# Values of the second tile ahead of the first up product, scores of the third tile behind the second: an attention and feed-forward kernel on one core

## The chip, the cores and the metric

The kernel runs on one core of a Trainium2 chip. The core has a matrix engine (TensorE, "PE" in the profile, its weight loads "PEld"), a vector engine (VectorE, DVE), an activation engine (ScalarE, ACT), a general engine (GpSimd, POOL) and a queue engine (SyncE, SP); 16 DMA engines move data. The metric is the device time of the program in microseconds (us). Before the change its median over 13 runs was 210.06 us (209.4 to 212.1).

## The reference

Chunked attention with a little context and eight memory slots, and behind it a layer norm and a two-layer feed-forward block with a residual:

```python
# q, k, v: (4, 8, 768, 64); mem_k, mem_v: (4, 8, 8, 64)
for c in range(24):                                    # chunks of 32 queries
    k_ctx = k[:, :, max(0, 32*c - 16) : min(768, 32*c + 40)]     # 16 left, 8 right; v_ctx alike
    k_full = concatenate([mem_k, k_ctx]); v_full = concatenate([mem_v, v_ctx])
    a = softmax(q_c @ k_full.T / 8)
    out[:, :, 32*c : 32*c + 32] = a @ v_full
x = out.transpose(0, 2, 1, 3).reshape(4, 768, 512)     # heads side by side
xn = (x - mean(x)) / sqrt(var(x) + 1e-6) * g_ln
return x + maximum(xn @ w_ch1, 0) @ w_ch2              # w_ch1 512 x 2048, w_ch2 2048 x 512
```

## The kernel before

**Tiles.** A tile is 128 rows of one batch element with all eight heads, so there are six tiles to a batch element and 24 in all, written `(b, t)`. Three tiles make a unit `u` of the feed-forward part (8 units). W1 and W2 lie in four quarters each (`w1c[0..3]`, `w2c[0..3]`).

**Steps of one tile.** `scores` (L319) does 16 small matmuls of keys (`KT`) against queries (`QR`) into an `att` slot of PSUM. `soften` (L335), twice, is the exponential on ScalarE into `AT`. `weigh` (L349) does 16 matmuls of `AT` with `V` into an `att` slot, with a column of ones that gives the sums of the softmax; `gather` (L361) takes reciprocals and scales on VectorE into `xs`, with the row sum beside it, and makes the negative mean; `values` (L345) is `weigh` and then `gather`. `norm` (L374) makes `xn` on VectorE. `turn_x` (L395) transposes `xn` on TensorE and copies it into `xT` with VectorE. `stats` and `root` find the reciprocal deviation, which is applied at the very end. `up_tile` (L453) multiplies one tile with one quarter of W1, `up_two` (L439) two tiles at once with one quarter, in two PSUM slots; `relu` (L420) takes each product out on ScalarE or VectorE. `down` (L470) multiplies with W2.

**Keys.** `transpose_block` brings a block of 256 keys, turned, into PSUM. `window` (L218) copies the piece of it that one group of 64 keys sees into `KT`, in two halves; pieces are numbered 0 to 3. Block 1 of batch element 0 (`K1`, L694) lies in the PSUM bank `mm[2]`. `key_left` (L199) copies the left context of a group from the group ahead of it. `half_q` and `part_q` turn half a block of queries and copy it to `QR`; `mix_q` (L285) puts the raw queries in order on VectorE beforehand. `v_mem` (L142) puts the memory values into `V`. `warm` (L591) issues matmuls on zeros that nobody uses.

**Order.** The order of each engine's instructions is written out by hand, and each engine follows it; a wait comes in only where data or a buffer is needed. PSUM slots of one kind are taken in turn (`slot`, L87): four of `mm`, two of `att`. The first unit starts by hand, in the lines that the change touches; from `plan` on (L776) steps are put on a time table. Behind the changed lines come: `up_two(0, 2)` with the third quarter, the products of tile 2 alone, and the loads' last parts.

**Loads.** POOL's queue issues nearly all loads, in the order of L662 to L690: `load_v(b, g)` one of twelve pieces of V, `load_w1(c)` a quarter of W1, `load_q(0, 1, h)` half a block of queries in two transfers. POOL's loads use eight semaphores in turn: a load waits until the eighth load before it has landed. SP's queue carries the transposing DMAs (`cross`, L306, and `turn_x` of most tiles) and the stores.

Of the kernel before, what the change touches and what calls it, by code (L numbers as in the profile page):

```python
# [15 lines left out]
def kernel(  # L16
# [67 lines left out]
    mm = [ps.tile([128, 512], FP32, name=f"mm{i}") for i in range(4)]  # L84
    turn = {"att": 0, "mm": 0}

    def slot(kind):  # L87
        lst = {"att": att, "mm": mm}[kind]
        turn[kind] = (turn[kind] + 1) % len(lst)
        return lst[turn[kind]]  # L90

    def dram(t, offset, pattern):
        return bass.AP(tensor=t.tensor, offset=offset, ap=[list(p) for p in pattern])

    def free(ap, off, pattern, parts=None):
        p = list(ap.ap[0]) if parts is None else [ap.ap[0][0], parts]
        return bass.AP(tensor=ap.tensor, offset=ap.offset + off, ap=[p] + [list(x) for x in pattern])

    def as16(t):
        return t.bitcast(FP16)  # L100

    def copy(eng, out, in_):
        if eng is nc.scalar:
            eng.copy(out=out, in_=in_)  # L104
        else:
            eng.tensor_copy(out=out, in_=in_)  # L106

    dve, act, pool = nc.vector, nc.scalar, nc.gpsimd
# [26 lines left out]
    def load_v(b, g):  # L135
        lo, hi = 16 if g == 0 else 0, 80 if g == NG - 1 else 96
        nc.gpsimd.dma_start(  # L137
            out=V[b % 2][lo:hi, g, :, 0:64],
            in_=dram(v, b * H * HS + (64 * g - 16 + lo) * D, [[64, hi - lo], [HS, H], [1, 64]]),
        )  # L140
# [7 lines left out]
    def load_w1(c):  # L148
        nc.gpsimd.dma_start(
            out=w1c[c], in_=dram(moe_w_ch1, 512 * c, [[FF, 128], [128 * FF, 4], [1, 512]])  # L150
        )
# [47 lines left out]
    def key_left(b, g, eng):  # L199

        copy(eng, free(KT[b % 2], GW * g, [[W, 4], [1, 16]]),
             free(KT[b % 2], GW * (g - 1) + 64, [[W, 4], [1, 16]]))
# [15 lines left out]
    def window(b, blk, banks, k0, eng):  # L218

        for half in ((0, 1) if eng is dve else (1, 0)):  # L220
            key_piece(b, banks[half], 4 * blk + k0, *PIECES[k0], eng, half)
# [63 lines left out]
    def mix_q(b, blk, half, eng):  # L285
        rows = slice(64 * half, 64 * half + 64)
        s, o = pick(st, ("b", b, blk, 1))[rows, :], pick(iv, ("b", b, blk, 1))[rows, :]
        copy(eng, free(o, 0, [[64, 2], [128, 8], [1, 64]]), s)
# [30 lines left out]
    def scores(b, t):  # L319
        p = slot("att")  # L320
        score_slot[b, t] = p
        for gg in range(2):
            for j in range(4):
                for par in range(2):
                    rows = slice(64 * par, 64 * par + 64)
                    nc.tensor.matmul(  # L326
                        out=p[:, par, (4 * gg + j) * 64 : (4 * gg + j) * 64 + 64],
                        lhsT=free(KR[b % 2][rows, :], GW * (2 * t + gg) + W * j, [[1, 128]]),
                        rhs=free(QR[b % 2][rows, t // 2, :, :], 8 * gg +
                                 (32 * j + 16 * (t % 2) if (b, t) >= (1, 4) else 64 * (t % 2) + 16 * j),  # L330
                                 [[128, 8], [1, 8]]),
                        start=True, stop=True, tile_position=(64 * par, 0),
                    )

    def soften(b, t, c):  # L335
        p = score_slot[b, t]
        nc.scalar.activation(  # L337
            out=free(AT[t % 3], 32 * c, [[64, 16], [1, 32]]),
            in_=free(p, 4 * c, [[64, 16], [1, 4], [8, 8]], W),
            func=ACTF.Exp, bias=band[0:W, c : c + 1], scale=0.125,  # L340
        )
# [3 lines left out]
    def values(b, t):  # L345
        weigh(b, t)
        gather(b, t)

    def weigh(b, t):  # L349
        p = value_slot[b, t] = slot("att")  # L350
        for par in range(2):
            for j in range(4):
                for gg in range(2):
                    nc.tensor.matmul(  # L354
                        out=p[64 * gg : 64 * gg + 64, par, 128 * j : 128 * j + HD],
                        lhsT=AT[t % 3][:, par, gg, j, :],
                        rhs=V[b % 2][:, 2 * t + gg, 4 * par + j, 0:HD],
                        start=(j == 0), stop=(j == 3), tile_position=(0, 64 * gg),
                    )

    def gather(b, t):  # L361
        p, r, x = value_slot[b, t], rec[t % 2], xs[(NT * b + t) % 9]
        nc.vector.reciprocal(out=r, in_=free(p, 64, [[128, 8]]))
        nc.vector.scalar_tensor_tensor(  # L364
            out=x.rearrange("p (h d) -> p h d", h=8),
            in0=free(p, 0, [[128, 8], [1, 64]]), scalar=1.0,
            in1=free(r, 0, [[1, 8], [0, 64]]),
            op0=ALU.mult, op1=ALU.mult, accum_out=tot[t],
        )
        nc.vector.tensor_scalar(  # L370
            out=nmean[t], in0=tot[t], scalar1=-1.0 / 512, scalar2=None, op0=ALU.mult
        )

    def norm(b, t, gb=gb):  # L374
        i = NT * b + t
        nc.vector.scalar_tensor_tensor(  # L376
            out=xn[i % 4], in0=xs[i % 9], scalar=nmean[t], in1=gb, op0=ALU.add, op1=ALU.mult,
        )
# [16 lines left out]
    def turn_x(b, t):  # L395
        i = NT * b + t
        dst = xT[(i // 3) % 2][:, :, 128 * (i % 3) : 128 * (i % 3) + 128]
        if i not in ON_PE:
            nc.sync.dma_start_transpose(out=dst, in_=xn[i % 4])
            return  # L400
        p = slot("att")
        pv = as16(p[:, 0, :])
        for dt in range(4):
            nc.tensor.matmul(  # L404
                out=pv[:, 128 * dt : 128 * dt + 128],
                lhsT=xn[i % 4][:, 128 * dt : 128 * dt + 128], rhs=identity,
                is_transpose=True, start=True, stop=True,
            )
        nc.vector.tensor_copy(out=dst, in_=free(pv, 0, [[128, 4], [1, 128]]))
# [29 lines left out]
    def up_two(u, c, engs):  # L439

        for m, eng in engs:
            p = slot("mm")
            for k_ in range(2):
                for dt in range(4):
                    nc.tensor.matmul(
                        out=p[:, 256 * k_ : 256 * k_ + 256],
                        lhsT=free(w1c[c][:, dt, :], 2 * m + k_, [[4, 128]]),
                        rhs=xT[u % 2][:, dt, 0:256],
                        start=(k_ == 0 and dt == 0), stop=(k_ == 1 and dt == 3),
                    )  # L450
            relu(eng, rT[c][:, 2 * m : 2 * m + 2, 0:256], free(p, 0, [[256, 2], [1, 256]]))

    def up_tile(u, c, i, eng):  # L453
        p = slot("mm")
        for k_ in range(4):
            for dt in range(4):
                nc.tensor.matmul(
                    out=p[:, 128 * k_ : 128 * k_ + 128],
                    lhsT=free(w1c[c][:, dt, :], k_, [[4, 128]]),
                    rhs=xT[u % 2][:, dt, 128 * i : 128 * i + 128],  # L460
                    start=(k_ == 0 and dt == 0), stop=(k_ == 3 and dt == 3),
                )
        pair = rT[c][:, :, 128 * i : 128 * i + 128], free(p, 0, [[128, 4], [1, 128]])
        if eng is None:
            return pair
        relu(eng, *pair)
# [124 lines left out]
    def warm(n, m=512, p=None):  # L591
        p = mm[3] if p is None else p
        for _ in range(n):
            nc.tensor.matmul(out=p[:, 0:m], lhsT=zero[:, 0:128], rhs=zero[:, 0:m], start=True, stop=True)
# [66 lines left out]

    load_v(0, 0)  # L662
    load_v(0, 1)
    load_w1(0)
    load_q(0, 1, 0)
    load_v(0, 2)
    load_v(0, 3)
    load_w1(1)
    load_v(0, 4)
    load_v(0, 5)  # L670
# [23 lines left out]
    K1 = [as16(mm[2])[:, 512 * h : 512 * h + 512] for h in range(2)]  # L694
# [46 lines left out]
    copy(act, gb, mm[3])  # L741
    warm(4, 512, mm[1])
    turn_x(0, 0)
    mix_q(0, 1, 0, dve)
    window(0, 1, K1, 0, act)
    window(0, 1, K1, 1, act)
    window(0, 1, K1, 2, dve)
    key_left(0, 4, dve)
    turn["mm"] = 3
    late = up_tile(0, 0, 0, None)  # L750
    Q1 = as16(slot("mm"))
    half_q(0, 1, 0, Q1)
    part_q(0, 1, 0, Q1, act)
    warm(1, 512, mm[3])
    scores(0, 2)
    values(0, 1)
    norm(0, 1)
    soften(0, 2, 0)
    soften(0, 2, 1)
    window(0, 1, K1, 3, act)  # L760
    warm(5, 512, mm[3])
    turn_x(0, 1)
    relu(dve, *late)
    v_mem(0, 4, 6, dve)
    total(cnt[:, 1:2], 0, 80)
    total(cnt[:, 2:3], 96, W)
    nc.vector.tensor_tensor(out=cnt[:, 1:2], in0=cnt[:, 1:2], in1=cnt[:, 2:3], op=ALU.add)
    up_tile(0, 0, 1, act)
    values(0, 2)
    up_two(0, 1, ((0, act), (1, act)))  # L770
    norm(0, 2)
    turn_x(0, 2)
    up_two(0, 2, ((0, act), (1, act)))
# [190 lines left out]
```

## Time and profile before

| What | us |
|---|---|
| median of 13 runs (range) | 210.06 (209.4 to 212.1) |
| the profiled execution, its span | 212.1, 210.3 |
| TensorE busy | 199.0 |
| VectorE busy | 163.1 |
| ScalarE busy | 109.9 |
| POOL busy | 110.3 |

All times inside the profile count from the start of the span. A timeline row gives the start, the busy time of a group of equal instructions, engine, line, operation, output and inputs, shapes and the number of instructions; in brackets the engine's idle time ahead of it and what ended it. Groups of several matmuls are pipelined, so the end of a group is a little behind the start of the next. A row of stages gives start and end, the length, the busy time of PE, PEld, DVE, ACT and POOL with the number of instructions, the granted clock of TensorE, the share of the DMA engines and their GB/s.

### The profile page before, as it was taken

The numbers are of one execution on the slowest core, as the hardware profiler recorded it, in microseconds if no ns is written. First come the engines' busy times: TensorE is split into PE (matmuls) and PEld (weight loads), VectorE is DVE, ScalarE is ACT, GpSimd is POOL, SyncE is SP. The second block draws the span as 40 slices with busy tenths as digits, with TensorE's granted clock in tenths as the row PEclk, the third lists the DMA queues.
The fourth block names the chain that finished last, engine by engine and source line by source line (L and its number), as shares of the span: only waits on it lengthen the run. The fifth ranks groups of instructions, "written<-read, shape, count | busy, mean of one in ns | idle before, by whom it ended". The sixth has DMA issues, their size and how long they took to land.

```text
span 210.3 us, 5284 instructions
## 1 busy us (share of the span) xinstructions
PE 199.0 (95%) x2045; PEld 135.0 (64%) x2045; DVE 163.1 (78%) x402; ACT 109.9 (52%) x238; POOL 110.3 (52%) x189
## 2 busy tenths in 40 slices
PE   7776999999999999989999999999999999999992
PEld 2454895547765467566666866586658766776581
DVE  5985836598989999968598999995897679565654
ACT  2764369637786077807693176737770566022300
POOL 7975787899789999733667893400040013000000
PEclk9999999999999999999999999999999999999999
DMA  5999999999999979998999999996022211220012
GB/s 157 200 193 191 212 198 185 202 148 235 162 131 155 184 160 129 130 157 227 162 152 171 95 199 131 117 199 154 1 48 79 100 27 28 78 100 0 0 53 100
DMA packets 74099, 28.11 MB, mean 134 GB/s; under 512 B 62169, under 2 KB 70105, under 8 KB 74074
## 3 DMA queue, kind: packets, MB, share of 16 engines
q0 software_dynamic: 46336, 14.71, 68.8%
q1 hardware_dynamic: 27594, 12.80, 28.9%
q10 hardware_dynamic: 144, 0.26, 0.5%
q8 instruction: 16, 0.26, 0.5%
q14 instruction: 9, 0.07, 0.1%
HBM read 30.28 MB, written 6.29 MB: 174 GB/s over the span
## 4 chain that ended last, share of the span: by engine, by line
PE 67%; DVE 5%; DMA 5%; ACT 2%; issue 1%; DVEq 0%
PE mm L430 33%; PE mm L475 14%; PE mm L522 13%; DMA QR<-iv 5%; PE att L354 3%; DVE osb L538 3%; PE att L326 2%; ACT AT L337 1%; DVE xs L364 1%; DVE KT L106 1%; PE att L404 1%; DVE three L492 0%; PE mm L233 0%; PE att L233 0%; ACT rT L422 0%
## 5 line engine op out<-in xcount | busy, mean ns | idle before, releaser
L430 PE MATMUL mm<-xT,w1c 128*128 128x384 f16 x464 | 81.1, 327 | 0.0
L422 ACT ACTIVATE rT<-mm 128x384 f16<-128x384 f32 (+1 forms) x78 | 38.6, 499 | 55.1 <-PE mm L430 48.4
L430 PEld LDWEIGHTS <-w1c 128*128 128x128 f16 x464 | 51.0, 114 | 21.1
L475 PE MATMUL mm<-w2c,rT 128*128 128x512 f16 x192 | 44.4, 379 | 0.0
L137 POOL DMA_DIRECT2D V<-in_v_dram x48 | 38.5, 809 | 5.0 <-DMA V<-in_v_dram 2.0
L424 DVE TENSOR_SCALAR rT<-mm 128x384 f16<-128x384 f32 (+1 forms) x47 | 26.1, 560 | 15.0 <-PE mm L430 11.8
L337 ACT ACTIVATE AT<-att,band 104x512 f16<-104x512 f32 x48 | 31.1, 686 | 3.4 <-PE att L326 3.2
L475 PEld LDWEIGHTS <-rT 128*128 128x128 f16 x192 | 18.2, 98 | 19.5
L387 POOL TENSOR_SCALAR veps<-sq 128x1 f32<-128x1 f32 x24 | 7.8, 327 | 43.3 <-ACT junk L381 21.3
L522 PEld LDWEIGHTS <-SA 128*128 128x128 f16 x184 | 17.9, 98 | 3.4 <-DVE SA L492 1.4
L381 ACT ACTIVATE junk<-xs,nmean 128x512 f16<-128x512 f32 x24 | 17.3, 720 | 4.5 <-issue 1.8
L123 POOL DMA_DIRECT2D st<-in_q_dram x28 | 16.2, 597 | 4.2 <-DMA st<-in_q_dram 2.0
L391 POOL TENSOR_TENSOR rstd<-veps,mhalf 128x1 f32<-128x1 f32 x24 | 16.5, 686 | 2.0
L364 DVE SCALAR_TENSOR_TENSOR xs<-att,rec 128x512 f32<-128x512 f32 x24 | 16.6, 692 | 0.9
L376 DVE SCALAR_TENSOR_TENSOR xn<-xs,nmean,gb 128x512 f16<-128x512 f32 x23 | 16.6, 747 | 0.2
L522 PE MATMUL mm<-T,SA 128*128 128x256 f16 x144 | 16.7, 273 | 0.0
L522 PEld LDWEIGHTS <-rT 128*128 128x128 f16 x144 | 14.1, 98 | 3.2 <-issue 0.3
L104 ACT COPY KT<-rawk 128x352 f16<-128x352 f16 (+2 forms) x14 | 10.3, 783 | 7.1 <-DMA rawk<-iv 7.1
L129 POOL DMA_DIRECT2D st<-in_k_dram x22 | 12.8, 592 | 0.8 <-DMA w2c<-in_moe_w_ch_dram 0.8
L522 PE MATMUL mm<-w2c,rT 128*128 128x256 f16 x96 | 12.4, 273 | 0.0
L106 DVE COPY iv<-st 128x1024 f16<-128x1024 f16 (+1 forms) x23 | 10.3, 454 | 1.9 <-DMA QR<-iv 1.6
L106 DVE COPY V<-memv 8x2560 f16<-8x2560 f16 (+1 forms) x14 | 10.8, 774 | 0.4
(107 smaller groups left out, 232.4 us busy)
## 6 DMA issues: line engine op xcount, KB each, us to landing
out_dram<-osb SPq DMA_DIRECT2D x23, 256.0 KB, 2.3
V<-in_v_dram POOLq DMA_DIRECT2D x40, 96.0 KB, 5.9
st<-in_k_dram POOLq DMA_DIRECT2D x22, 128.0 KB, 5.2
w1c<-in_moe_w_ch_dram POOLq DMA_DIRECT2D x4, 512.0 KB, 8.1
st<-in_q_dram POOLq DMA_DIRECT2D x32, 64.0 KB, 4.9
w2c<-in_moe_w_ch_dram POOLq DMA_DIRECT2D x4, 512.0 KB, 8.7
st<-in_q_dram POOLq DMA_DIRECT2D x6, 128.0 KB, 8.1
V<-in_v_dram POOLq DMA_DIRECT2D x8, 80.0 KB, 5.4
```

The costliest lines, as they stand in the source:

```text
L106: eng.tensor_copy(out=out, in_=in_)
L137: nc.gpsimd.dma_start(out=V[b % 2][lo:hi, g, :, 0:64], in_=dram(v, b * H * HS + (64 * g - 16 + lo) * D, [[64, hi - lo], [HS, H], [1, 64]]),)
L337: nc.scalar.activation(out=free(AT[t % 3], 32 * c, [[64, 16], [1, 32]]), in_=free(p, 4 * c, [[64, 16], [1, 4], [8, 8]], W), func=ACTF.Exp, ...
L364: nc.vector.scalar_tensor_tensor(out=x.rearrange("p (h d) -> p h d", h=8), in0=free(p, 0, [[128, 8], [1, 64]]), scalar=1.0, in1=free(r, 0, ...
L376: nc.vector.scalar_tensor_tensor(out=xn[i % 4], in0=xs[i % 9], scalar=nmean[t], in1=gb, op0=ALU.add, op1=ALU.mult,)
L381: nc.scalar.activation(out=junk, in_=xs[(NT * b + t) % 9], func=ACTF.Square, bias=nmean[t], scale=1.0, accum_out=sq[t],)
L391: nc.gpsimd.tensor_tensor(out=rstd[(NT * b + t) % 9], in0=veps[t % 3], in1=mhalf, op=ALU.pow)
L422: nc.scalar.activation(out=o, in_=p, func=ACTF.Relu)
L424: nc.vector.tensor_scalar(out=o, in0=p, scalar1=0.0, scalar2=None, op0=ALU.max)
L430: nc.tensor.matmul(out=p, lhsT=free(w1c[c][:, dt, :], i, [[4, 128]]), rhs=xT[u % 2][:, dt, 128 * lo : 128 * (lo + n)], start=(dt == 0), st ...
L475: nc.tensor.matmul(out=p, lhsT=rT[c][:, k_, 128 * i : 128 * i + 128], rhs=w2c[c][:, k_, :], start=(c == 0 and k_ == 0), stop=(c == 3 and k ...
L522: nc.tensor.matmul(out=p, lhsT=left(h)[:, k_, :], rhs=right(h)[:, k_, :], start=(h == 0 and k_ == 0), stop=(h == 1 and k_ == 3),)
```

## The change

Tile 1's V loads (pieces 2 and 3) are issued ahead of the first quarter of W1 and of the queries. On TensorE tile 1's `weigh` comes right after the transpose of tile 0, ahead of tile 0's up product; its `gather` and `norm` follow on VectorE directly after `mix_q`. The six filler matmuls around become three. `turn_x(0, 1)` comes ahead of tile 2's scores. Window 2 of block 1 and `key_left` move behind the copy of `turn_x(0, 1)` on VectorE, and window 3 on ScalarE comes ahead of tile 2's softens. Tile 2's scores and softens move behind tile 1's up product. `values(0, 2)` moves behind `up_two(0, 1)`, whose second relu moves from ScalarE to VectorE. Nothing else is changed, and what is computed is the same.

```diff
     load_v(0, 0)
     load_v(0, 1)
+    load_v(0, 2)
+    load_v(0, 3)
     load_w1(0)
     load_q(0, 1, 0)
-    load_v(0, 2)
-    load_v(0, 3)
     load_w1(1)
...
     turn_x(0, 0)
+    weigh(0, 1)
     mix_q(0, 1, 0, dve)
+    gather(0, 1)
+    norm(0, 1)
     window(0, 1, K1, 0, act)
     window(0, 1, K1, 1, act)
-    window(0, 1, K1, 2, dve)
-    key_left(0, 4, dve)
     turn["mm"] = 3
     late = up_tile(0, 0, 0, None)
     Q1 = as16(slot("mm"))
     half_q(0, 1, 0, Q1)
     part_q(0, 1, 0, Q1, act)
-    warm(1, 512, mm[3])
-    scores(0, 2)
-    values(0, 1)
-    norm(0, 1)
-    soften(0, 2, 0)
-    soften(0, 2, 1)
+    warm(3, 512, mm[3])
+    turn_x(0, 1)
+    window(0, 1, K1, 2, dve)
+    key_left(0, 4, dve)
     window(0, 1, K1, 3, act)
-    warm(5, 512, mm[3])
-    turn_x(0, 1)
     relu(dve, *late)
     v_mem(0, 4, 6, dve)
...
     up_tile(0, 0, 1, act)
+    scores(0, 2)
+    soften(0, 2, 0)
+    soften(0, 2, 1)
+    up_two(0, 1, ((0, act), (1, dve)))
     values(0, 2)
-    up_two(0, 1, ((0, act), (1, act)))
     norm(0, 2)
     turn_x(0, 2)
     up_two(0, 2, ((0, act), (1, act)))
```

## The prediction, made before the changed kernel ran

> **What bounds the kernel now.** I read the shares by engine first, then busy time by stage, then the timeline of the stage that the edit touches, then TensorE's later waits.
>
> ```profile
> PE 199.0 (95%) x2045; PEld 135.0 (64%) x2045; DVE 163.1 (78%) x402; ACT 109.9 (52%) x238; POOL 110.3 (52%) x189
> ...
> 15.00:22.00 7.00, 4.89 (x81) 3.43 (x81) 4.43 (x13) 3.39 (x10) 4.30 (x8) 1.00 1.45 195
> 22.00:30.00 8.00, 7.82 (x115) 7.32 (x114) 4.49 (x13) 4.17 (x7) 6.22 (x9) 1.00 1.36 204
> ```
>
> The second and third lines are stages (start:end, length, then busy us of PE, PEld, DVE, ACT, POOL, the clock, DMA). From 22 us on PE is full, and it does its instructions in the order written. So what counts is when it begins the unbroken stretch: I take the start of `up_two(0, 2)`, the second group of L445, as the marker. Whatever delays it delays the rest, unless a later wait of PE swallows it. Behind the first 15 us only the stage to 22 us has holes to speak of, 2.1 us of them, and 1.6 us of what is busy are filler matmuls (L594).
>
> ```profile
> 14.41 0.39 PE L404 MATMUL att<-identity,xn 128*128 128x128 f16 x4
> 14.83 0.42 DVE L409 COPY xT<-att 128x512 f16<-128x512 f16 x1 [0.26 <-PE att L404]
> 15.31 1.05 PE L457 MATMUL mm<-xT,w1c 128*128 128x128 f16 x16 [0.52 <-DVE xT L409]
> 16.20 0.59 DVE L106 COPY KT<-mm 128x176 f16<-128x176 f16 x2 [0.49 <-ACT KT L104]
> 17.37 0.41 PE L326 MATMUL att<-QR,KT 64*128 64x64 f16 x16 [0.35 <-ACT QR L104]
> 17.71 0.44 PE L354 MATMUL att<-V,AT 104*64 104x65 f16 x16
> 18.23 0.21 DVE L363 RECIPROCAL rec<-att 128x8 f32<-128x8 f32 x1 [1.35 <-PE att L354]
> 18.98 0.48 ACT L104 COPY KT<-mm 128x160 f16<-128x160 f16 x2
> 20.20 0.40 PE L404 MATMUL att<-identity,xn 128*128 128x128 f16 x4 [0.86 <-DVE xn L376]
> 21.19 1.08 PE L457 MATMUL mm<-xT,w1c 128*128 128x128 f16 x16 [0.59 <-DVE xT L409]
> 22.30 0.44 PE L354 MATMUL att<-V,AT 104*64 104x65 f16 x16
> 22.68 1.94 PE L445 MATMUL mm<-xT,w1c 128*128 128x256 f16 x16
> 22.79 0.21 DVE L363 RECIPROCAL rec<-att 128x8 f32<-128x8 f32 x1
> 24.77 0.40 PE L404 MATMUL att<-identity,xn 128*128 128x128 f16 x4
> 25.00 1.91 PE L445 MATMUL mm<-xT,w1c 128*128 128x256 f16 x16
> ```
>
> Two chains are to be seen. Tile 1: values on PE (17.71), then VectorE's reciprocal to `xn` (18.23 to 20.14, 1.91 us), transpose (20.20), copy, up product (21.19). PE has little but filler meanwhile. Tile 2: the same chain, from 22.30 to the transpose at 24.77, has the 1.94 us of `up_two(0, 1)` laid over it, so PE loses only about 0.3 us. The 16.20 row is one more reading: VectorE's window copy waited for ScalarE's, which reads the same PSUM bank.
>
> ```profile
> 83.22 2.51 SPq L309 DMA_TRANSPOSE QR<-iv  x1
> ...
> 93.07 0.43 DVE L106 COPY iv<-st 128x1024 f16<-128x1024 f16 x1 [1.63 <-DMA QR<-iv]
> ...
> 94.75 1.05 PE L522 MATMUL mm<-w2c,SA 128*128 128x256 f16 x8 [1.08 <-DVE SA L492]
> ...
> 99.42 0.29 PE L326 MATMUL att<-QR,KT 64*128 64x64 f16 x8 [0.35 <-DVE KT L106]
> ```
>
> These are the places where a shift could shrink: a transposing DMA that took 9.73 us holds VectorE, and PE then waits 1.08 and 0.35 us (0.16 us besides, at 62.67, for ScalarE, which is itself paced by PE).
>
> **The loads.** V loads 2 and 3 go ahead of W1's first quarter and the two loads of q. POOL's issue times (0.79 each) put W1(0) at 5.74 + 1.57 = 7.31 us, the q loads at 8.1; from W1(1) on the order is as before. The five transfers landed at 13.04 (W1(0)), 13.5 and 13.83 (q), 14.4 and 14.9 (V). They follow each other closely, so I take the stream as the limit: V 2 and 3 now land near 11.3, W1(0) 1.07 later, at 14.1, and q last, at 14.9. The other end is the issue delay itself: 14.6 and 15.4. W1(0) is wanted at 15.34, q by `mix_q` at 15.29. Cost: nothing, at most 0.15 us on VectorE; the cover is the wait for `xT`, and without it all later starts move one for one. POOL's loads wait each for the eighth before: W1(2) now waits for V 2 instead of W1(0), so it is issued about 1.5 us before 13.38. It landed at 21.3 behind W1(1) and V 4 and 5 (18.7), and PE wants it at 25: no gain, and no loss. W1(3) still waits for W1(1). SP's queue is not touched.
>
> **Tile 1's values forward.** `weigh(0, 1)` needs tile 1's weights, which ScalarE ends at 14.91: 14.96 to 15.34, before `up_tile(0, 0, 0)`, which started at 15.31 anyway: 0.03 us. VectorE does the copy of `xT` to 15.25 and `mix_q` to 15.71, then tile 1's chain, 1.91 us: `xn` at 17.65 instead of 20.14. PE does up product, `half_q` and three fillers (to about 17.4), transposes at 17.71, and the copy of `xT` begins 0.51 us later (20.20 to 20.71), at 18.22. A lead of 2.49 us so far; three fillers fewer (0.7 us) are part of it, not added to it.
>
> **The moved windows.** `window(0, 1, K1, 2)` and `key_left` now stand behind that copy on VectorE. K1 lies in mm[2], the bank that `up_tile(0, 0, 1)` takes. So PE must wait for window 3 on ScalarE, and window 3 for window 2 on VectorE, as the 16.20 row shows for one bank. 18.22 + 0.34 (next start after such a copy, 20.71 to 21.05) = 18.56; window 2 takes 0.59, window 3 0.48, hand-overs 0.05 each: PE starts at 19.73. Without this PE would start at 18.70. Of the lead 1.46 us is left (19.73 against 21.19).
>
> **Tile 2 behind.** `up_tile` occupies PE 1.11 us (21.19 to 22.30), the scores 0.34 (17.37 to 17.71): `up_two(0, 1)` at 21.18, still 1.50 ahead. ScalarE's relu (0.60) and the two softens (1.27) end near 22.75; `weigh(0, 2)` comes 1.75 after 21.18, at 22.93, uncovered by them. Now the tile 2 chain has nothing over it: next on PE is `turn_x(0, 2)`, which wants `xn`. And VectorE must first do the second relu of `up_two(0, 1)`, which moved to it from ScalarE: products end at 21.18 + 1.94 = 23.12, relu 0.69 (L424, this form 0.68 to 0.69) to 23.84, chain 1.92 (22.79 to 24.71) to 25.76, transpose at 25.82, `up_two(0, 2)` 0.23 later at 26.05. Before: 25.00. **So +1.05 us**, and PE stands idle about 2.5 us before the transpose. VectorE's starts overlap by up to 0.08 us; over three or four of them the low end is +0.75. The high end, with q at 15.4 and a late soften, is +1.5. Nothing else is behind the relu on VectorE that PE wants sooner.
>
> **What is left at the end.** From 26 us all of PE's order is the same. At 94 us: the transposes that hold VectorE start with VectorE's own work and so 1.05 later; the V loads beside them (76.73 to 87) come from POOL, which does not wait for PE there. If the DMA engines only lose what they had free when the first transpose came late (POOL issues a V each 0.79, they landed some 0.5 apart where the stream was full), the landing moves by about a third, 0.35 us, and PE's waits swallow 0.7. If it moves fully, nothing. I take 0.25 swallowed, nearer the second, since the profiled execution (212.1 us, span 210.3) is the slowest of 13 and the median, 210.06, may not have that wait at all. Net +0.8: span 211.1, an execution like the profiled one 212.9, median 210.06 + 0.8 = 210.86. The Trainium skill, "DMA: Bandwidth & Descriptors", Queues, rings and completion order, says that each DMA engine serves its queues in turn, packet by packet. By that a later transpose still shares with the V loads and lands fully later: the sum would be +1.05. The rows (9.73 us here, 3.1 and 3.8 at other places) do show the sharing, not its shares.
>
> **The clock.** The first ten fillers took 4.45 us (0.43 apart), four at 13.53 took 1.04 (0.22 apart), though the clock column reads full throughout. The change opens holes of about 1.6 us (18.0 to 19.73) and 2.5 us. A longer hole than 1.2 us is not in this trace, so the price lies between nothing and half of such a slow stretch, 4.4 / 2 = 2.2 us. I take nothing, nearer the holes of 0.5 to 1.1 us, after which the next groups had their usual length. The Trainium skill, "TensorE: Matmul & The Clock Gate", Why this matters for your kernels, warns of idle gaps above about 3 us between bursts: by it neither hole alone slows the array and the sum stays.
>
> **Rivals.**
> 1. Swallowed: the transposing DMA lands where it did, PE's 1.43 us of waits at 94 and 99 take the shift. Time 210.1 (+0 to +0.35). For it: the DMA column at 9 there. Against: the transposes are issued later.
> 2. Faster: the later transposes miss the V loads, and PE's later waits go altogether (1.59 us): 1.05 - 1.59 = -0.54, with the low end of the shift -0.84: about 209.4. It decides when the 9.73 us falls below 8.7, so that QR lands earlier than 92.95. Against it: twelve V loads are still landing until 94.4.
> 3. The clock falls in the second hole: +0.8 + 2.2, 213.1.
> 4. W1(0) or q later than thought, past 15.4: one for one, +1.3 to +1.8, 211.6.
>
> **How the numbers follow.** No change can be told within 0.3% (0.63 us). My forecast 0.63 (+0.4 to +1.3 us; 0.48 of it above the bound, 0.15 within), rival 1 0.14, rival 2 0.13, rival 3 0.06, rival 4 0.04. Faster 0.13, same 0.15 + 0.14 = 0.29, slower 0.48 + 0.06 + 0.04 = 0.58. The range goes from part of rival 2, 209.7, to past the high end of the shift, 211.9; it leaves out the clock and the deep end of rival 2. The forecast's own range is 210.4 to 211.4.
>
> **What would show it.** Right: L354 of tile 1 near 15.0, the second L404 near 17.7, the second L457 near 19.7 with a wait for ScalarE's KT copy; L404 of tile 2 near 25.8 after an idle time of 2 to 2.5 us for `xn`, and `up_two(0, 2)` near 26. Wrong: `up_two(0, 2)` before 25.0, L457's groups waiting on w1c's DMA, L445 rows of more than 0.3 us each, or an end that does not follow the marker, which the rows at 94 us would explain.

## The result, and the profile after

The changed kernel took 212.92 us in the median (11 runs, 211.79 to 216.95), the kernel before 210.1 beside it (48 runs, 209.38 to 213.47). The ratio is 1.0126, with an interval of 1.0099 to 1.0153: slower by 1.3%, and above the predicted range. (The ratios here leave out the most disturbed executions of either kernel; medians, ranges and clocks are over all runs.) The profiled execution of the changed kernel took 212.47, its span 210.7.

The page's line of busy time and two rows of stages, after (columns as before):

```profile
PE 198.3 (94%) x2042; PEld 134.5 (64%) x2042; DVE 163.8 (78%) x403; ACT 108.8 (52%) x237; POOL 110.3 (52%) x189
...
15.00:22.00 7.00, 5.33 (x87) 4.34 (x82) 4.77 (x16) 3.56 (x11) 3.83 (x7) 1.00 1.45 193
22.00:30.00 8.00, 5.76 (x92) 5.32 (x91) 4.38 (x10) 2.95 (x6) 6.23 (x10) 1.00 1.36 203
```

TensorE is busy 5.76 us of the 8 from 22 us on, where it was busy 7.82 before. The timeline of TensorE and VectorE, after, shows both holes:

```profile
14.19 0.39 PE L404 MATMUL att<-identity,xn 128*128 128x128 f16 x4
14.74 0.44 PE L354 MATMUL att<-V,AT 104*64 104x65 f16 x16 [0.17 <-ACT AT L337]
15.12 1.08 PE L457 MATMUL mm<-xT,w1c 128*128 128x128 f16 x16
...
17.44 0.40 PE L404 MATMUL att<-identity,xn 128*128 128x128 f16 x4
...
18.21 0.58 DVE L106 COPY KT<-mm 128x176 f16<-128x176 f16 x2
18.82 0.49 ACT L104 COPY KT<-mm 128x160 f16<-128x160 f16 x2 [1.66 <-DVE KT L106]
19.36 1.05 PE L457 MATMUL mm<-xT,w1c 128*128 128x128 f16 x16 [1.53 <-ACT KT L104]
20.69 1.94 PE L445 MATMUL mm<-xT,w1c 128*128 128x256 f16 x16
22.55 0.44 PE L354 MATMUL att<-V,AT 104*64 104x65 f16 x16
22.66 0.69 DVE L424 TENSOR_SCALAR rT<-mm 128x512 f16<-128x512 f32 x1 [2.10 <-PE mm L445]
23.27 0.20 DVE L363 RECIPROCAL rec<-att 128x8 f32<-128x8 f32 x1
25.23 0.40 PE L404 MATMUL att<-identity,xn 128*128 128x128 f16 x4 [2.24 <-DVE xn L376]
25.47 1.91 PE L445 MATMUL mm<-xT,w1c 128*128 128x256 f16 x16
```

The first hole, 1.53 us, is the shared bank: VectorE's window, then ScalarE's, then the product (18.21, 18.82, 19.36). The second, 2.24 us, is tile 2's chain with nothing over it (22.66 to 25.23). The marker, the second L445 row, is at 25.47 instead of 25.00. The chain starts earlier here, though: counted from tile 0's transpose the marker comes after 11.28 us (25.47 - 14.19) instead of 10.59, so 0.69 us later. At 84 to 100 us, after:

```profile
83.76 2.62 SPq L309 DMA_TRANSPOSE QR<-iv  x1
...
93.51 0.43 DVE L106 COPY iv<-st 128x1024 f16<-128x1024 f16 x1 [1.53 <-DMA QR<-iv]
...
95.18 1.05 PE L522 MATMUL mm<-w2c,SA 128*128 128x256 f16 x8 [1.01 <-DVE SA L492]
...
99.83 0.29 PE L326 MATMUL att<-QR,KT 64*128 64x64 f16 x8 [0.32 <-DVE KT L106]
```

Both waits of TensorE are still there: 1.01 + 0.32 for 1.08 + 0.35. I call this the late wait.

So this one pair of profiles says +0.4 us (span 210.7 against 210.3), and the medians say +2.8. What the profiled execution doesn't show is in the clocks of the others: its mean granted clock was 1.000, but of the 12 executions on record (one, of 210.42 us, is not among the 11 of the median) nine had 0.996 or less (0.972 the lowest, with 216.95 us). Of the 104 runs of the kernel before that stood beside the experiments below, 25 had. The three with 1.000 took 212.47 (with the late wait, by its profile), 212.45 and 210.42.

A mean just below 1 is no proof of a loss, though. In the profiles of e1, e6, e7, e8, e10, e11, e13 and e14 (means of 0.995 to 0.998) the clock reads 1.00 until the last matmul has ended, and 0.50 only behind it, where it costs nothing. Two rows of stages, e1, whose last matmuls end at 204.8:

```profile
150.00:207.00 57.00, 54.72 (x485) 38.82 (x483) 39.15 (x88) 20.84 (x46) 5.65 (x12) 1.00 0.18 55
207.00:208.00 1.00, 0.00 (x0) 0.00 (x0) 0.00 (x0) 0.00 (x0) 0.00 (x0) 0.56 0.18 62
```

A fall of the length that e2 shows below (3.4 us at half) takes 0.008 off the mean. Clocks of 0.992 or less were five of the 12, and six of the 104. The four executions at 0.996 may have lost nothing by the clock.

My theory from here on (the clock): the holes cost little themselves, but TensorE's clock falls behind them in most executions. The rivals: the loads (W1 or q late), and the late wait, which the shift might have made more frequent.

### The profile page after: what moved, and what is told of

It reads as the page before. It is cut to its first block, busy times and chain, and to the rows that moved or that the text cites. A ratio compares the mean times of both kernels' runs of the same rounds, so it can differ in the third digit from the quotient of the medians.

```text
span 210.7 us, 5279 instructions
## 1 busy us (share of the span) xinstructions
PE 198.3 (94%) x2042; PEld 134.5 (64%) x2042; DVE 163.8 (78%) x403; ACT 108.8 (52%) x237; POOL 110.3 (52%) x189
## 4 chain that ended last, share of the span: by engine, by line
PE 67%; DVE 5%; DMA 5%; ACT 2%; issue 1%; DVEq 0%
PE mm L430 33%; PE mm L475 14%; PE mm L522 13%; DMA QR<-iv 5%; PE att L354 3%; DVE osb L538 3%; PE att L326 2%; ACT AT L337 1%; DVE xs L364 1%; PE att L404 1%; DVE KT L106 0%; DVE three L492 0%; PE mm L233 0%; PE att L233 0%; ACT rT L422 0%
## 5 line engine op out<-in xcount | busy, mean ns | idle before, releaser
L422 ACT ACTIVATE rT<-mm 128x384 f16<-128x384 f32 (+1 forms) x77 | 37.8, 497 | 54.5 <-PE mm L430 47.5
L424 DVE TENSOR_SCALAR rT<-mm 128x384 f16<-128x384 f32 (+1 forms) x48 | 26.8, 562 | 17.2 <-PE mm L430 11.9
L387 POOL TENSOR_SCALAR veps<-sq 128x1 f32<-128x1 f32 x24 | 7.1, 294 | 44.4 <-ACT junk L381 22.5
L123 POOL DMA_DIRECT2D st<-in_q_dram x28 | 15.7, 570 | 2.8 <-DMA st<-in_k_dram 2.3
L522 PEld LDWEIGHTS <-rT 128*128 128x128 f16 x144 | 14.1, 98 | 3.1 <-issue 0.2
L129 POOL DMA_DIRECT2D st<-in_k_dram x22 | 13.4, 616 | 1.0 <-DMA w2c<-in_moe_w_ch_dram 0.9
```

The source lines that it names most:

```text
L422: nc.scalar.activation(out=o, in_=p, func=ACTF.Relu)
L424: nc.vector.tensor_scalar(out=o, in0=p, scalar1=0.0, scalar2=None, op0=ALU.max)
L522: nc.tensor.matmul(out=p, lhsT=left(h)[:, k_, :], rhs=right(h)[:, k_, :], start=(h == 0 and k_ == 0), stop=(h == 1 and k_ == 3),)
```

## The experiments

Four groups, each on one chip with its own runs of the kernel before. For the length of the changed stretch I count from the start of `up_tile(0, 0, 0)` (first L457) to the start of the L457 group of 32, behind the marker: 11.44 us before (15.31 to 26.75), 12.09 after (15.12 to 27.21).

**Group 1.** Fillers (`warm`, matmuls on zeros that nobody uses) put over both holes, over the second alone, and taken away in the kernel before; and the loads alone.

e1_fill_both, against the changed kernel:

```diff
     turn_x(0, 1)
+    warm(6, 512, mm[3])
...
     values(0, 2)
+    warm(9, 512, mm[1])
     norm(0, 2)
```

> The changed kernel with six filler matmuls in the first hole of TensorE (behind the transpose of tile 1, about 1.3 us of filler) and nine in the second (behind tile 2's values, about 1.9 us). Theory A: the profile explains only about 0.7 us of the 2.8 us (the marker up_two(0, 2) came 0.47 us later than before, with a start 0.22 us earlier); the rest is TensorE's clock, which the runs of the changed kernel show at 0.972 to 0.996 on the mean in ten executions of twelve. Then the fillers bring the clock back to 1.000 in nearly all executions, and the median falls to 210.5 to 211.2. Theory B: the order itself costs it, in executions unlike the profiled one (a transfer that is late in most of them), and the clock is a companion: the median stays at 212.5 to 213.3.

Measured: 211.32 (210.4 to 212.3, 12 runs), ratio 1.0032 [1.0006, 1.0057], median clock 0.998, two of the 12 at 0.992 or less. (The expectation says ten executions of twelve; by the record it is nine.) TensorE's timeline, e1:

```profile
17.21 1.46 PE L594 MATMUL mm<-zero 128*128 128x512 f16 x6
18.90 1.05 PE L457 MATMUL mm<-xT,w1c 128*128 128x128 f16 x16 [0.23 <-ACT KT L104]
...
22.47 2.12 PE L594 MATMUL mm<-zero 128*128 128x512 f16 x9
24.78 0.40 PE L404 MATMUL att<-identity,xn 128*128 128x128 f16 x4 [0.19 <-DVE xn L376]
```

The stretch is as long as after (12.16 us, the order's cost is all there), but the time is back to 0.3% above before. So 0.65 us is the order (with the new loads), and the other 2 us go when there is something in the holes. The late wait is also gone from this profile, so it alone doesn't part the two theories.

e2_fill_second, against the changed kernel:

```diff
     values(0, 2)
+    warm(9, 512, mm[1])
     norm(0, 2)
```

> The changed kernel with fillers in the second hole alone (nine, behind tile 2's values; PE idle there falls from 2.24 us to about 0.3). Theory A, if the longer hole is what lowers the clock: as with both holes filled, 210.5 to 211.2, clock 1.000. If the two holes count together as too little work in a stretch: part of it, 211.2 to 212.3, with some executions under 1.000. Theory B: 212.5 to 213.3.

Measured: 213.51 (213.29 to 213.72, 4 runs), 1.0121 [1.0076, 1.0166]; clocks 0.991, 0.998, 0.991, 0.989. The timeline and a row of stages, e2:

```profile
19.10 1.05 PE L457 MATMUL mm<-xT,w1c 128*128 128x128 f16 x16 [1.53 <-ACT KT L104]
20.57 3.39 PE L445 MATMUL mm<-xT,w1c 128*128 128x256 f16 x16
```

```profile
20.00:25.00 5.00, 5.00 (x55) 3.30 (x53) 1.20 (x6) 2.35 (x4) 3.33 (x6) 0.66 1.24 205
```

Here the fall can be seen: about 1 us behind the end of the 1.53 us hole the clock goes down. It is 0.66 in the mean of five microseconds (at 0.50 that is 5 x 0.34 / 0.5 = 3.4 us of it), and the same 16 matmuls take 3.39 us instead of 1.94. The second hole is not needed for it. Whether the first one alone is enough is less sure: in the three profiles with a fall behind it TensorE had waited for tile 1's `xn` just ahead of it (e2 0.47, e9 0.73, e15 0.26 us), in the two with this hole and no fall behind it less (e16 0.20, the profile after nothing that its row shows). The time is above all ranges of the expectation; this execution also has the late wait, 1.03 us.

e4_before_no_fill, against the kernel before, whose order and output stay as they are:

```diff
     part_q(0, 1, 0, Q1, act)
-    warm(1, 512, mm[3])
     scores(0, 2)
...
     window(0, 1, K1, 3, act)
-    warm(5, 512, mm[3])
     turn_x(0, 1)
```

> The kernel before without its six fillers between half_q and tile 1's transpose (one ahead of tile 2's scores, five behind tile 1's values). No chain is changed; TensorE gets a hole of about 2.1 us from 18.1 to 20.2 and one of 0.6 us behind it. Theory A: the clock falls below 1.000 in a good part of the executions and the median rises by 0.5 to 2.5 us, to 210.6 to 212.6. Theory B: nothing waits for fillers, 209.8 to 210.4, clock 1.000.

Measured: 212.77 (211.35 to 215.52, 12 runs), 1.0099 [1.0064, 1.0134]; all 12 clocks were 0.992 or less, median 0.9855. The timeline and the stages by microsecond, e4:

```profile
19.48 0.40 PE L404 MATMUL att<-identity,xn 128*128 128x128 f16 x4 [2.04 <-DVE xn L376]
22.27 3.04 PE L445 MATMUL mm<-xT,w1c 128*128 128x256 f16 x16
```

```profile
20.00:21.00 1.00, 0.54 (x10) 0.54 (x11) 1.00 (x2) 0.00 (x0) 0.06 (x1) 1.00 1.23 199
21.00:22.00 1.00, 1.00 (x22) 0.80 (x21) 0.90 (x5) 0.20 (x1) 0.68 (x2) 0.59 1.23 201
22.00:23.00 1.00, 1.00 (x18) 0.76 (x13) 0.61 (x3) 0.40 (x1) 1.00 (x2) 0.50 1.25 208
23.00:24.00 1.00, 1.00 (x7) 0.69 (x6) 0.93 (x4) 0.00 (x0) 1.00 (x3) 0.50 1.25 214
24.00:25.00 1.00, 1.00 (x8) 0.82 (x7) 0.33 (x1) 0.60 (x1) 0.74 (x1) 0.70 1.23 198
```

This is the cleanest of them: no order and no load is changed, nothing depends on what is taken away, and the kernel loses 1.0%. Its profile has the clock at 0.50 for about 3.4 us behind holes of 2.04 and 0.59 us (the second, ahead of the product at 20.46, is in the kernel before too). The six fillers of the kernel before, 1.6 us of work that looks like waste, are worth 2.1 us.

e5_loads_only is the kernel before with the diff's first part alone:

```diff
     load_v(0, 1)
+    load_v(0, 2)
+    load_v(0, 3)
     load_w1(0)
     load_q(0, 1, 0)
-    load_v(0, 2)
-    load_v(0, 3)
```

> The kernel before with the loads alone reordered (V pieces 2 and 3 ahead of W1's first quarter and of q). Theory A: W1's first quarter lands near 14.1, before it is wanted at 15.3, the same time within 0.3 us, 209.8 to 210.4. Theory B, if the loads are what is late in most executions: 211 to 213, with L457 waiting for w1c's DMA.

Measured: 210.6 (209.45 to 212.7, 10 runs), 1.0021 [0.9984, 1.0057]. The profile has VectorE waiting 0.52 us for q, and no wait for W1. No loss that can be told, though the interval allows up to 0.6% (1.2 us); e1, which has the same loads, puts them and the order together at 0.65 us. So the loads by themselves are not where 2 us went. Four of the ten clocks here were 0.992 or less, however, against six of the 104 of the kernel before: the new order of loads may bring falls too, though this profile shows none before the last matmul.

**Group 2.** The first hole filled alone, and the two places in the order mended one at a time.

e3_fill_first, against the changed kernel:

```diff
     turn_x(0, 1)
+    warm(6, 512, mm[3])
     window(0, 1, K1, 2, dve)
```

> The changed kernel with fillers in the first hole alone (six, behind the transpose of tile 1); the second hole, 2.2 us ahead of tile 2's transpose, stays. With fillers in the second hole alone the clock still fell, at 20 us, ahead of that hole, so the first hole lowers it there. Theory A1: the second hole lowers it too, in a part of the executions: median 211.6 to 212.8, clock under 1.000 in half of them or more, the slow matmuls behind 25 us. Theory A2: only the first hole does it (with the fillers taken out ahead of it): as with both filled, 211.0 to 211.6.

Measured: 213.96 (213.32 to 215.31, 4 runs), 1.016 [1.0127, 1.0193]; clocks 0.992, 1.000, 0.989, 0.992. Its profiled execution is no witness for the second hole: the 2.24 us hole is there, but `up_two(0, 2)` behind it took 1.91 us at full clock; the low clock of that execution lay in its first 15 us (0.89), behind a wait of 1.07 us that ended at 6.12, and it has the late wait (1.24 and 0.21 us). Another of the four took 214.09 us at a clock of 1.000, so about 3 us were lost there without a fall, and no trace shows to what. The time is above both ranges of the expectation. What the run says is that the first hole's filling alone gains nothing; that the second hole's clock is the reason is not shown.

e6_window_ahead, against the changed kernel: window 2 goes ahead of the copy again, with fillers in what is left of the holes:

```diff
     warm(3, 512, mm[3])
-    turn_x(0, 1)
     window(0, 1, K1, 2, dve)
     key_left(0, 4, dve)
+    turn_x(0, 1)
+    warm(3, 512, mm[3])
...
     values(0, 2)
+    warm(9, 512, mm[1])
```

> The changed kernel with fillers in both holes (three and nine), and window 2 and key_left ahead of tile 1's copy on VectorE instead of behind it, where VectorE waits about 0.5 us for TensorE. Theory: the shared bank costs about 0.8 us; from the start of up_tile(0, 0, 0) to up_tile(0, 0, 2) it takes 11.2 to 11.4 us (before 11.44, changed kernel 12.09), and the time is that of the kernel before, ratio 0.996 to 1.001. Rival: tile 2's chain bounds it anyway, 12.0 us and a ratio as with both holes filled, 1.003.

Measured: 210.59 (209.44 to 211.52, 10 runs), 0.9987 [0.996, 1.0013]. `up_tile(0, 0, 1)` starts without a wait:

```profile
18.57 1.05 PE L457 MATMUL mm<-xT,w1c 128*128 128x128 f16 x16
```

From tile 1's transpose to this product it is 1.01 us (17.56 to 18.57) against 1.92 in e1 (16.98 to 18.90): the bank's order was worth 0.91 us. The stretch, 11.71 us against 12.16, shows only 0.45 of it (expected were 11.2 to 11.4), since VectorE waited 0.56 us for q here and tile 1's transpose came 0.47 us later behind the first product than in e1.

e7_product_ahead leaves the windows where the change put them, and lays `up_two(0, 2)` over tile 2's chain (with six fillers behind `turn_x(0, 1)` as in e1):

```diff
     values(0, 2)
+    up_two(0, 2, ((0, act), (1, act)))
+    warm(2, 512, mm[3])
     norm(0, 2)
     turn_x(0, 2)
-    up_two(0, 2, ((0, act), (1, act)))
+    warm(2, 512, mm[3])
```

> The changed kernel with fillers (six in the first hole, two and two around tile 2's transpose) and up_two(0, 2), which needs tiles 0 and 1 alone, ahead of tile 2's transpose, so that it covers tile 2's chain. Theory: the uncovered chain costs about 1 us; from up_tile(0, 0, 0) to up_tile(0, 0, 2) 11.0 to 11.3 us (before 11.44, changed kernel 12.09), ratio 0.994 to 1.000. Rival: the copy behind the transpose is what comes late next and takes it back: 11.6 us or more, ratio over 1.000.

Measured: 210.08 (209.56 to 212.19, 10 runs), 0.9973 [0.9945, 1.0001]. The stretch is 11.23 us: 0.93 less than e1. So the uncovered chain and the bank cost about the same (0.93 and 0.91).

e8_both_ahead does both, gives the second relu of `up_two(0, 1)` back to ScalarE, and needs fewer fillers (against the changed kernel):

```diff
-    turn_x(0, 1)
     window(0, 1, K1, 2, dve)
     key_left(0, 4, dve)
+    turn_x(0, 1)
+    warm(3, 512, mm[3])
...
-    up_two(0, 1, ((0, act), (1, dve)))
+    up_two(0, 1, ((0, act), (1, act)))
     values(0, 2)
+    up_two(0, 2, ((0, act), (1, act)))
+    warm(1, 512, mm[3])
     norm(0, 2)
     turn_x(0, 2)
-    up_two(0, 2, ((0, act), (1, act)))
+    warm(2, 512, mm[3])
```

> Both orders together (window 2 and key_left ahead of tile 1's copy; up_two(0, 2) ahead of tile 2's transpose), the second relu of up_two(0, 1) back on ScalarE, fillers in what is left (three, one and two). Theory: all that the change brings forward is kept: from up_tile(0, 0, 0) to up_tile(0, 0, 2) 9.9 to 10.3 us (before 11.44), clock 1.000 in most executions, ratio 0.991 to 0.996. Rival: the DMA stream is what bounds behind 30 us, then the marker comes early and the end does not: ratio 0.997 to 1.002, with new waits of TensorE behind 30 us.

Measured: 209.39 (208.65 to 211.36, 12 runs), 0.9954 [0.9928, 0.9981]; median clock 1.000. TensorE's timeline, e8:

```profile
18.63 1.05 PE L457 MATMUL mm<-xT,w1c 128*128 128x128 f16 x16
...
22.27 1.94 PE L445 MATMUL mm<-xT,w1c 128*128 128x256 f16 x16
...
25.29 1.95 PE L457 MATMUL mm<-xT,w1c 128*128 128x128 f16 x32 [0.15 <-DVE xT L409]
```

The stretch is 10.19 us, 1.25 less than before, and the ratio makes 0.97 us of it (0.0046 of 210.77). The changed order is a gain once it neither holds a bank nor uncovers the next chain. How much of that gain is tile 1's values, and how much `up_two(0, 2)` ahead of tile 2's transpose, is not shown: no run puts `up_two(0, 2)` ahead in the kernel before.

**Group 3.** The late wait. One of the copies (`mix`) that VectorE does ahead of the transposing DMAs is put three steps later on the time table, so that VectorE isn't held by `QR` when TensorE wants `SA`:

```diff
-                at(w, (3, 9, 18)[blk] + which, mix, b, blk, which, dve)
+                at(w, (3, 9, 18)[blk] + (4 if blk == 2 else 1) * which, mix, b, blk, which, dve)
```

It is done to the changed kernel (e9), to the kernel before (e10), to e8 (e11) and to e1 (e12).

> The changed kernel with one VectorE copy (mix(b, 2, 1), for b of 2 and 3, the one that waited 1.53 us for the transposing DMA near 93 us) three steps later, behind four VectorE operations that PE waits for. Theory S: the changed kernel loses to that wait more often than the kernel before (with the clock's loss taken off, about half of its executions lie some 1.5 us above the other half), so the ratio falls from 1.0126 to 1.005 to 1.010 and what stays is order (about 0.65 us) and clock. Theory C: order and clock are all there is, the ratio stays at 1.011 to 1.015, with PE's wait near 95 us gone from the profile all the same.

> The kernel before with the same copy three steps later. Theory S: the kernel before has that wait in a few executions alone, so it gains little, ratio 0.996 to 1.000, and fewer executions lie above 211.5 us. Theory C: the same, 0.999 to 1.001.

> Window 2 and up_two(0, 2) ahead with fillers in what is left, and the copy three steps later. Without the copy moved the ratio was 0.9954. Theory S: 0.990 to 0.995. Theory C: 0.994 to 0.997.

> The changed kernel with fillers in both holes, and the copy three steps later. With neither clock nor the late wait left, what stays is the order: 0.4 to 0.8 us over the kernel before with the copy moved, by both theories; its distance to the changed kernel with the copy moved is the clock's share, 0.5 to 1.5 us.

| Kernel | median (range), runs | ratio | stretch |
|---|---|---|---|
| e9: changed, copy later | 213.87 (211.73 to 215.5), 6 | 1.0123 [1.0076, 1.0169] | 16.02 |
| e10: before, copy later | 209.87 (209.6 to 211.14), 12 | 0.9981 [0.9955, 1.0007] | 11.79 |
| e11: e8, copy later | 208.81 (208.37 to 209.03), 6 | 0.9914 [0.9884, 0.9944] | 10.82 |
| e12: e1, copy later | 211.22 (210.32 to 214.24), 12 | 1.003 [1.0008, 1.0052] | 13.68 |

In all four profiles the waits at 94 and 99 us are gone. The changed kernel loses 1.2% all the same, with clocks of 0.981, 0.981, 1.000, 0.990, 0.982 and 0.981. Its profile, e9, has a fall behind each hole; the stages:

```profile
20.00:23.00 3.00, 3.00 (x34) 2.29 (x32) 0.58 (x4) 1.81 (x3) 1.91 (x3) 0.50 1.24 202
23.00:27.00 4.00, 1.76 (x28) 1.32 (x27) 2.41 (x6) 0.60 (x1) 3.03 (x6) 0.93 1.22 213
27.00:30.00 3.00, 3.00 (x17) 2.19 (x17) 1.37 (x3) 0.60 (x1) 2.80 (x4) 0.50 1.59 189
```

So a loss of this size does not need the late wait. Whether the late wait adds to the changed kernel's loss in other executions these runs don't tell: e9 and the changed kernel ran on different chips, and only a profiled execution shows the wait. By their ratios e9 fits theory C, e10 and e11 fit S; e12 lies about 1.0 us above e10 and 2.0 below e9, both more than expected (0.4 to 0.8, and 0.5 to 1.5).

The profiles do say when the wait appears. Among the 13 with the copy in its old place, the L457 group of 32 began after 27 us in six (after, e2, e3, e4, e15, e16), and all six have it, 0.43 to 1.45 us in all. Of the seven where it began earlier only two have it (before 1.43, e7 0.51). So a TensorE that is late by the order, by a fall or by a load seems to bring the late wait with it. That is a pattern of 13 executions, not a proof.

The profile of e12 (213.63 us, one of its two long ones) brings something else, the loads:

```profile
15.90 1.08 PE L457 MATMUL mm<-xT,w1c 128*128 128x128 f16 x16 [1.30 <-DMA w1c<-in_moe_w_ch_dram]
16.84 0.42 DVE L106 COPY iv<-st 64x1024 f16<-64x1024 f16 x1 [2.39 <-DMA st<-in_q_dram]
```

In this execution W1's first quarter came 1.30 us and q 2.39 us late, and the clock was at 0.50 from 18 to 21 us, with both holes filled: here it fell behind the waits for loads. e9 waited 0.39 and 1.27 us, e11 0.84 for q.

e11 is the fastest kernel of the study, 1.53 us under the kernel before beside it.

**Group 4.** Does the wait for q matter? `mix_q` is put behind tile 1's `gather`, and `half_q` and `part_q` behind the three fillers, so that a late q holds nothing of tile 1's chain; done to the changed kernel (e15), to e1 (e13) and to e11 (e14). With them the changed kernel once more, unaltered (e16).

```diff
     weigh(0, 1)
-    mix_q(0, 1, 0, dve)
     gather(0, 1)
+    mix_q(0, 1, 0, dve)
     norm(0, 1)
...
     late = up_tile(0, 0, 0, None)
     Q1 = as16(slot("mm"))
+    warm(3, 512, mm[3])
     half_q(0, 1, 0, Q1)
     part_q(0, 1, 0, Q1, act)
-    warm(3, 512, mm[3])
```

> The same with fillers in both holes. With fillers alone the ratio was 1.003 twice. Theory Q: 0.999 to 1.002. Theory N: 1.002 to 1.004.

> The fastest version so far (window 2 and up_two(0, 2) ahead, fillers in what is left, one later copy near 93 us; ratio 0.9914), with mix_q behind tile 1's gather. In its profile VectorE waited 0.84 us for q. Theory Q: 0.987 to 0.991. Theory N: 0.990 to 0.993.

> The changed kernel with mix_q, which waits for q's DMA, behind tile 1's gather instead of ahead of it on VectorE, and the three fillers ahead of half_q; no fillers in the holes. Theory Q (the late load of q costs some 0.5 us in the typical execution, which begins tile 0's chain 0.6 us earlier than the first profile): ratio 1.007 to 1.012, some 0.5 us below the changed kernel, clocks as low as there. Theory N: as the changed kernel, 1.010 to 1.015.

> The changed kernel itself, beside the three others on one chip. Both theories: ratio 1.010 to 1.015, most clocks under 0.997. Theory Q: in its profile VectorE waits 0.2 to 1.3 us for q's DMA ahead of tile 1's gather, as it does in eight of ten profiled executions of kernels with the new order (0.22 to 2.39 us), though not in the changed kernel's first profile. Theory N: no such wait, the first profile is typical.

| Kernel | median (range), runs | ratio | clocks |
|---|---|---|---|
| e13: e1, q late | 210.53 (210.28 to 212.28), 12 | 1.0023 [0.9995, 1.005] | median 0.998 |
| e14: e11, q late | 209.06 (208.23 to 210.06), 12 | 0.9941 [0.9914, 0.9968] | median 0.9975 |
| e15: changed, q late | 215.0 (211.29 to 215.88), 6 | 1.0123 [1.0046, 1.0201] | 0.984 four times, 0.992, 0.998 |
| e16: changed, unaltered | 216.09 (212.93 to 216.91), 8 | 1.0294 [1.0265, 1.0323] | all 0.992 or less, median 0.984 |

Taking q off the chain changes nothing that can be told: e13 against e1 and e12 (1.0032, 1.003), e14 against e11 (0.9914), each pair on two chips with overlapping intervals (e14's ratio is above both ranges of its expectation). e15 keeps its holes, and loses as the changed kernel does; its profile has L445 at 3.36 and 3.43 us.

e16 is the direct witness: the changed kernel itself, caught with a fall. TensorE's timeline and the stages, e16:

```profile
24.86 0.61 PE L404 MATMUL att<-identity,xn 128*128 128x128 f16 x4 [2.23 <-DVE xn L376]
25.26 3.20 PE L445 MATMUL mm<-xT,w1c 128*128 128x256 f16 x16
```

```profile
25.00:26.00 1.00, 1.00 (x8) 0.81 (x7) 0.42 (x1) 0.00 (x0) 0.17 (x1) 0.50 1.28 212
26.00:27.00 1.00, 1.00 (x7) 0.69 (x6) 0.85 (x2) 0.00 (x0) 0.47 (x1) 0.50 1.15 222
27.00:28.00 1.00, 1.00 (x7) 0.74 (x6) 0.00 (x0) 0.60 (x1) 1.00 (x2) 0.56 1.08 218
28.00:29.00 1.00, 1.00 (x18) 1.00 (x16) 0.00 (x0) 0.51 (x1) 0.96 (x3) 1.00 1.64 151
```

The marker group takes 3.20 us where it took 1.91 in the profile after: 1.29 us more. There is no wait for W1 or q in this execution, and the first hole, as long as ever (1.53 us), did not lower the clock in it. Whether a hole brings a fall differs from one execution to the next. The whole stretch took 13.61 us, 1.52 more than in the profile after; the late wait is there too (0.99 and 0.21 us). This was the profile of one of the faster executions of e16, 213.38 us. The median, with a clock of 0.984, is what two falls would leave, and the ratio of 1.0294 is above the range of both theories.

## Why the prediction was wrong

The steps in their order:

- **The loads: "nothing, at most 0.15 us".** Right for the profiled execution after, where nothing waited for W1 or q (they landed at 13.9 and 14.6, ahead of the predicted 14.1 and 14.9), and e5 alone shows no loss. The limit was too tight: of the twelve profiled executions with the new order of loads (without e13 to e15, where q is used later) seven waited 0.2 to 2.4 us for q, and two (e9, e12; besides them e13) 0.39 to 1.30 us for W1. I had taken 15.3 us for the time they are wanted from one execution; in 11 of the 16 experiments tile 0's product started at 14.4 to 14.8. The old order is not free of this either: e10, with its loads as before, waited 0.45 us for q. That the waits for q cost time in the median is not shown (e13, e14).
- **Tile 1's values forward.** Right: `weigh` directly behind the transpose (14.74), the second transpose 3.25 us behind the first one, predicted 3.30.
- **The moved windows.** Right: transpose to product 1.92 us, predicted 2.02, with the wait for ScalarE's copy as described. e6 confirms the cause.
- **Tile 2 behind.** The mechanism was right (e7), the size a little high: from `up_tile(0, 0, 1)` to the marker 6.11 us instead of 6.32, since the next start came before the end ahead of it (the reciprocal at 23.27, the relu's end at 23.35). Relu to transpose took 2.57, not 2.70, and `up_two(0, 1)` came 1.33 behind `up_tile(0, 0, 1)`, not 1.45. Counted from tile 0's transpose the shift was 0.69, not 1.05, just under the low end of 0.75.
- **The end: 0.25 swallowed.** 0.10 was (1.43 to 1.33). "The V loads come from POOL, which does not wait for PE there" was wrong: batch 2's began at 77.27 instead of 76.73, moved by 0.54 (TensorE by 0.51 at 63 us), behind a copy of `xT` on POOL that moved as much, so the transposing DMA met the same company. For this pair of profiles too little to matter: 0.69 - 0.10 gives 0.6 us net, 0.3%, which is what e1, e12 and e13 measure with the holes filled (1.0032, 1.003, 1.0023). But only a late wait that shrinks was reckoned with; that a later TensorE might bring it into executions that had none was put at nothing. The 13 profiles of Group 3 speak for it, without showing its size in the median.
- **The clock: "I take nothing".** This is the step that failed. I had both holes (about 1.6 and 2.5 us; measured 1.53 and 2.24) and the bound, 2.2 us, and chose the lower end because holes of 0.5 to 1.1 us had done no harm. That was the wrong nearest row: falls followed holes of 2.24 (e9), 2.04 (e4) and 1.53 us (e2), and in e3 even one of 1.07 us near the start. A fall costs 1.3 to 1.5 us on the marker's kind of group (3.20 and 3.39 for 1.91 and 1.94), and 1.7 us in all if TensorE is busy throughout (half of 3.4 us), which takes 0.008 off the mean clock of a span of 211. The row quoted from the Trainium skill ("TensorE: Matmul & The Clock Gate", Why this matters for your kernels), gaps above about 3 us, does not bound the falls in this kernel; the measured ones behind 1.53 us (e2) and 2.04 us (e4) decide.

Rival 3, the clock falling in the second hole, 213.1 us, had the right mechanism, with a chance of 0.06. That its time lies 0.2 us from the median is luck: its 2.2 us came from slow fillers at the start, one fall costs 1.7, and the median clock of 0.996 stands for 0.8 us at most (0.004 of 211). It left out that the first hole does it too, that it is a matter of chance per execution, and the late wait. The sign for it that I had named, longer L445 rows, was absent from the profile after and present in e2, e4, e9, e15 and e16. The signs named for being right (the five starts and the 2.24 us hole) all stood in the profile after, somewhat early; the loss lay in executions that this profile is not.

In sum: of the 2.8 us between the medians 0.6 to 0.7 is the order, as predicted to within 0.2. The other 2 us go when the holes are filled (e1), and appear when the kernel before is given such holes (e4). That the clock falls behind the holes is shown. Its share of the 2 us is open: by the median clock of the first chip it is 0.8 us at most, and what is then left, about 1.3 us, has the size of one late wait (1.33 us in the profile after), which no run shows for the median execution.

## What to carry to other kernels

A hole on TensorE of 1.5 to 2.2 us inside a busy stretch can cost more than its length: here a fall of the clock to half for about 3.4 us followed in some, and on one chip probably in all: clocks of 0.992 or less in five of 12 executions on the first chip, in all eight on the other. Price each new hole with it, and lay independent products (e8) or, failing that, unused matmuls (e1) over it. Before a step is moved, ask what it had lain under: a product over a chain is cover for the chain, and a copy out of a PSUM bank stands before the next product into that bank. Read the clocks of all executions beside the profile: the profiled one here was one of three in twelve with a full clock. Then look where the clock was low: behind the last matmul it costs nothing.

## What the runs showed of the hardware that was not expected

- The same changed kernel lost 1.3% on one chip and 2.9% on another (1.0126 and 1.0294, intervals apart), with median clocks of 0.996 and 0.984: by the clocks of 0.992 or less (five of 12, eight of eight) the same holes brought falls more often in the second case.
- Filling one of two holes gained nothing (e2 and e3, 1.0121 and 1.016; for e3 the traces do not show why), filling both gained 0.9%.
- In eight profiles the clock fell only behind the last matmul, and the mean clock of the execution read 0.995 to 0.998 for it.
- Taking out unused matmuls made the kernel slower (e4, 2.1 us for 1.6 us of fillers).
- In one execution (e12) the same loads landed about 2 us later than in the profile after: waits of 1.30 us for W1 and 2.39 us for q, where the profile after has none.
